# Second products with tokens stationary in the 768-token tiles, four low halves per tile on GpSimd, and the cubic term in another instruction form

## The chip, the core and the metric

The kernel runs on one core of one Trainium2 chip. The metric is device time in microseconds (us), from the start of the program to its end, as the median of several runs; the profile adds one execution seen instruction by instruction.

## The reference, cut to what matters

2,304 tokens of width 512 come out of a local and global attention (4 batches, 8 heads, 512 local and 32 global tokens each) and go through two feed-forward layers with 2,048 hidden units. The change touches the second layer.

```
x = moe(attention(...))                       # layer 1: h = relu(x @ w_in); x = (h*h) @ w_out
h = x @ w_in                                  # layer 2, (2304, 512) @ (512, 2048)
P = a[0] + a[1]*h + a[2]*h*h + a[3]*h*h*h
Q = 1.0 + |b[0]|*|h| + |b[1]|*h*h
out = (P / (Q + 1e-6)) @ w_out                # (2304, 2048) @ (2048, 512)
```

## The kernel before

Each float32 number that enters TensorE is split into a high half (rounded to the fp32r type) and a low half (the remainder), and each product is made of three matmuls: high by high, high by low, low by high.

Most of the tokens of both layers are worked in six tiles (SUMMED): three in layer 1 and three in layer 2, of 768, 768 and 640 tokens (numbers 3, 4 and 5 of the list). A tile's first product, x @ w_in, is a Strassen-like scheme: seven products M1 to M7 of half-size blocks (`product`, line 438), whose moving operands are seven sums of blocks of the tile, named A11, A12, S2, S1, S3, A22 and S4. `sides` makes those sums, their high halves (ScalarE, line 336) and their low halves (VectorE, line 339), a step at a time, for the next tile while the present one is worked. The last four low halves are those of S1, S3, A22 and S4. A tile has eight rounds (q, NPAIR of them; s counts them over all tiles), each for two chunks (f) of 128 hidden units. The program of a round is written out by hand in `step_a` to `step_d`: the products M1; M2 and M6; M5 and M7; M4 and M3. They go to two banks of PSUM, s0 and s1. After each of these four steps, `groups` puts in one part of the second product of an earlier round (six parts, one and a half rounds, late).

VectorE adds the parts of the seven products together (lines 627, 659 and 684: one operand in SBUF, one in PSUM, and the bank can be written again when they have read it), and it does most of the rational function of the round before (lines 547 to 572): `below`, `cube`, `above`, `error`, `ratio`, `refine`, and `glow`, which makes the low half of the result for the second product. These instructions read both inputs from SBUF. ScalarE does the squares, the logarithm and exponential for the division, the high halves and many copies out of PSUM. GpSimd in layer 2 does no arithmetic: it issues the fetches (`fetch`, line 416) of the weight blocks of the round after next, each of which waits until TensorE has read the block that it overwrites. The order on each engine is the order of the program.

The second product, g @ w_out (`blocks`, line 465), accumulates a whole tile over 16 chunks. In tiles 3 and 4, as in layer 1, the weight is the stationary operand and the tokens move: for each of four strips of 128 output columns, a matmul over 512 tokens and one over 256, in the banks tc0, tc1, pv0, pv1 (512) and s2, s3 (two pieces of 256 each); three matmuls to each piece, 24 to a chunk, in two parts. `leave` then copies eight pieces out of PSUM, on ScalarE for these tiles, and four DMAs write the tile to the output with columns and tokens transposed; the host puts it right. In the last tile (5) the tokens are the stationary operand, 128 at a time, and all 512 output columns of the weight move: five rows of 128 tokens, three matmuls of 512 columns each, in tc0, tc1, pv0, pv1 and s2; `depart` copies each row out and writes it.

Of the kernel before, what the change touches and what calls it, by code (L numbers as in the profile page):

```python
# [11 lines left out]
F32 = mybir.dt.float32  # L12
# [5 lines left out]
ALU = mybir.AluOpType  # L18
# [4 lines left out]
DM, DFF = 512, 2048  # L23
NTOK = B * (SL + SG)
# [13 lines left out]
KD, KF = DM // 128, DFF // 128  # L38
# [3 lines left out]
SUMMED = [(512, 256), (1024, 256), (1536, 320), (0, 384), (768, 384), (1536, 320)]  # L42
NPAIR = KF // 2
LAST = len(SUMMED) - 1
# [38 lines left out]

def body(ctx, tc, qT, kW, v, w1i, w1o, w2i, w2o, coef, out):
    nc = tc.nc
    cut = SUMMED[LAST][0]
    out_t = out[:cut * DM].rearrange("(p d c) -> p d c", p=128, d=KD)
    out_r = out[cut * DM:].rearrange("(n c) -> n c", c=DM)
    pe, act, dve, pool, sync = nc.tensor, nc.scalar, nc.vector, nc.gpsimd, nc.sync

    assert nc.sbuf_base <= BASE
# [4 lines left out]
    def at(name, off, *shape, dt=F32):  # L96

        assert off % 16 == 0 and off + int(np.prod(shape)) <= END * (2 if dt == I64 else 1)
        uses[name] = uses.get(name, 0) + 1
        return nc.alloc_sbuf_tensor_at(f"{name}_{uses[name]}", [128, *shape], dt, offset=BASE + 4 * off)[:]  # L100

    class Ring:
# [5 lines left out]
        def next(self):  # L108
            self.turn += 1
            return self.all[(self.turn - 1) % len(self.all)]  # L110
# [6 lines left out]
    x = at("x", 0, KD, NTOK)  # L117
# [19 lines left out]
    s_ps = [ps.tile([128, 512], F32, name=f"s{j}") for j in range(4)]  # L137
# [3 lines left out]
    acc_bank = tc_ps + pv_ps  # L141
# [148 lines left out]
    got = [[at("got", W0 + 8960 + 3584 * i + a, b - a, dt=F32R) for a, b in zip(CUTS, CUTS[1:])] for i in range(2)]  # L290
# [30 lines left out]
    def halves(t, part):  # L321
        p = pieces(t)
        n = len(p) // 2
        return p[n * part:n * part + n]

    def side(c, t, k):
        return sides_b[t][SLOTS[t][c]][k]

    def sides(t):

        c0, n = SUMMED[t]
        p11, p12, p21, p22 = (x[:, 2 * k:2 * k + 2, c0 + i * n:c0 + i * n + n] for i in range(2) for k in range(2))
        f = side("S2", t, 2)

        def high(c, src):
            act.activation(side(c, t, 0), src, AF.Copy)

        def low(c, src):
            dve.tensor_tensor(side(c, t, 1), src, side(c, t, 0).bitcast(F32), op=ALU.subtract)

        def sub(o, a, b, op=ALU.subtract):
            dve.tensor_tensor(o, a, b, op=op)

        high("A11", p11)
        yield
        low("A11", p11)
        yield
        sub(p11, p11, p21)
        high("A12", p12)
        yield  # L350
        low("A12", p12)
        yield
        sub(f, p22, p11)
        yield
        sub(p21, p21, p22, ALU.add)
        high("S2", f)
        yield
        sub(p12, p12, f)
        yield
        low("S2", f)  # L360
        yield
        high("S1", p21)
        high("S3", p11)
        low("S1", p21)
        yield
        high("A22", p22)
        low("S3", p11)
        yield
        high("S4", p12)
        low("A22", p22)  # L370
        yield
        low("S4", p12)
        yield

    def sides_now(t):

        c0, n = SUMMED[t]
        p11, p12, p21, p22 = (x[:, 2 * k:2 * k + 2, c0 + i * n:c0 + i * n + n] for i in range(2) for k in range(2))
        f = side("S2", t, 2) if t < 3 else at("sf", RAW + 7680, 2, n)
        src = {"A11": p11, "A12": p12, "S2": f, "S1": p21, "S3": p11, "A22": p22, "S4": p12}  # L380

        def high(c):
            act.activation(side(c, t, 0), src[c], AF.Copy)

        def low(c):
            dve.tensor_tensor(side(c, t, 1), src[c], side(c, t, 0).bitcast(F32), op=ALU.subtract)

        def sub(o, a, b, op=ALU.subtract):
            dve.tensor_tensor(o, a, b, op=op)

        def early():
            high("A11")
            yield
            low("A11")
            yield
            sub(p11, p11, p21)
            high("A12")
            yield
            low("A12")
            yield  # L400
            sub(f, p22, p11)
            yield
            sub(p21, p21, p22, ALU.add)
            yield
            sub(p12, p12, f)
            high("S2" if t < 3 else "S4")
            yield
            low("S2" if t < 3 else "S4")
            yield

        return early(), high, low
# [27 lines left out]
                          skip_group_check=True)  # L439

    def rows(t):
        return acc_bank + s_ps[2:4 if SUMMED[t][1] == 384 else 3]

    def part_of(t, part):
        return (range(3), range(3, len(rows(t))))[part]

    def blocks(q, f, part):

        t, u = divmod(q, NPAIR)
        j = u + NPAIR * f  # L450
        gh, gl = gq[q, f]
        w = w_out[j]
        assert have[1, j] == (q >= Q2)
        if t < LAST:
            pp = halves(t, part)
            ops = [(dst, w[:, a, 128 * d:128 * d + 128], b[:, o0:o1], first and i == 0, i == 2)
                   for d, o0, o1, dst, first in pp for i, (a, b) in enumerate(((0, gh), (1, gh), (0, gl)))]
        else:
            ops = [(rows(t)[k], b[:, 128 * k:128 * k + 128], w[:, a], i == 0, i == 2)
                   for k in part_of(t, part) for i, (a, b) in enumerate(((0, gh), (1, gh), (0, gl)))]  # L460
            if q == NQ - 1:
                order = ((0, 1, 3, 4, 6, 7, 2, 5, 8), (0, 1, 2, 3, 4, 6, 7, 5, 8))[f] if part == 0 else (0, 1, 3, 4, 2, 5)
                ops = [ops[i] for i in order]
        for dst, a, b, first, final in ops:
            pe.matmul(dst, a, b, start=first and j == 0, stop=j == KF - 1 and final, skip_group_check=True)  # L465
        if part == 1 and t == 2:
            freed.add(j)
        if j == KF - 1:
            (leave if t < LAST else depart)(t, part)
        for work in after.pop((q, f, part), ()):  # L470
            work()

    def leave(t, part):
        c0 = SUMMED[t][0]
        for k, (d, o0, o1, src, _) in enumerate(halves(t, part)):
            dst = x[:, d, c0 + o0:c0 + o1]
            if k % 2 == 0 and not (t in (3, 4) or t == 2 and part == 1):
                dve.tensor_copy(dst, src)
            else:
                act.activation(dst, src, AF.Copy)  # L480
            if t >= 3 and k % 2 == 1:
                sync.dma_start(out_t[:, d, c0:c0 + o1], x[:, d, c0:c0 + o1])

    def depart(t, part):
        c0, n = SUMMED[t]
        for k in part_of(t, part):
            rest = x[:, :, c0 + 512:c0 + 2 * n]
            o = x[:, k, c0:c0 + 512] if k < 4 else rest[:, 2 * (k - 4):2 * (k - 4) + 512 // (2 * n - 512)]
            i, r = rows(t)[k], out_r[128 * k:128 * k + 128]
            if k >= 4:  # L490
                i, r = (b.rearrange("p (a b) -> p a b", b=2 * n - 512) for b in (i, r))
            if t == len(SUMMED) - 1 and k % 2:
                dve.tensor_copy(o, i)
            else:
                act.activation(o, i, AF.Copy)
            (act if t == len(SUMMED) - 1 and k == len(rows(t)) - 1 else sync).dma_start(r, o)

    b2, b3 = 4 * Q2, 4 * NQ
    plan = {(Q2, 1): (), (Q2, 2): (b2 + 1,), (Q2, 3): (b2 + 2, b2 + 3),
# [7 lines left out]
    def group(i):  # L507
        i -= 6
        if i == 4 * Q2:
            return  # L510
        q, r = divmod(i - (i > 4 * Q2), 4)
        if 0 <= q < NQ:
            blocks(q, *divmod(r, 2))
# [19 lines left out]
    def ew(q, f):  # L533
        return [e[:, :2 * half(q)] for e in ea[f]] + [strip(q, 2 + f), strip(q, f)]
# [13 lines left out]

    def cube(q, f):
        a, b, t, h = ew(q, f)  # L550
        dve.tensor_tensor(t, t, h, op=ALU.mult)  # L551

    def above(q, f):
        a, b, t, h = ew(q, f)
# [28 lines left out]
    def step_a(s, tick):  # L583
# [16 lines left out]
        if two:  # L600
            linear(p, 0)
            cube(p, 0)
# [10 lines left out]
        if two:  # L613
            above(p, 0)
            below(p, 1)
            if not lagging(s):
                cube(p, 1)
            logexp(p, 0)
# [315 lines left out]
    with tc.manual_schedule():  # L934
# [12 lines left out]
        for a in range(2):  # L947
            h = m[64 * a:64 * a + 64]
# [6 lines left out]
        for b, r, c in ((0, 64, 0), (2, 0, 0), (3, 64, 128)):  # L955
            o = 32 * (b % 2)
# [504 lines left out]
        first, high, low = sides_now(0)  # L1461
# [48 lines left out]
        for q in range(1, Q2):  # L1510
            t, u = divmod(q, NPAIR)
            if q == NPAIR:
                spend(0.1)
            for k, step in enumerate((step_a, step_b, step_c, step_d)):
# [10 lines left out]
                if (u, k) == ((6, 0) if t < 2 else (5, 1)):  # L1525
                    if t:
                        clear(*((5, 6, 7) if t == 1 else (8, 9, 10, 1, 2, 3)))
                    early, high, low = sides_now(t + 1)
# [16 lines left out]
                if t == 0:  # L1545
# [4 lines left out]
                    while convs and (q, k) >= open_from[0] and owed > 0:  # L1550
                        c = next(convs[0], None)
# [96 lines left out]
```

## Time and profile before

| | |
|---|---|
| Median of 3 runs | 836.68 us (836.37 to 836.82) |
| The profiled execution | 836.86 us, of which the span shown is 835.1 us |
| TensorE (PE) busy | 827.8 us, 99% |
| VectorE (DVE) busy | 710.7 us, 85% |
| ScalarE (ACT) busy | 637.3 us, 76% |
| GpSimd (POOL) busy | 187.6 us, 22% |
| Granted clock of TensorE | 1.00 |

Busy time is what the profiler records for instructions; a matmul's recorded time overlaps with that of the next, so the pace of TensorE is read from starts, not from busy time. The profiled execution is 1.8 us longer than its span, and 0.18 us longer than the median.

### The profile page before, as it was taken

The page shows a single profiled execution, that of the slowest core. Times are in us where ns is not written, and L with a number is a line of the kernel's source. Part 1 is how long each engine was busy: PE and PEld are TensorE (multiplying, and loading weights), DVE is VectorE, ACT ScalarE, POOL GpSimd, SP SyncE. Part 2 cuts the span into 40 slices and gives each one's busy share as a digit, 9 for nine tenths or more (in the row PEclk, how much of TensorE's full clock was granted, in tenths as well). Part 3 has the DMA queues.
Part 4 walks back from the last instruction along what each step waited for, and adds up shares of the span by engine and source line. Part 5 has one row for each costly group of instructions (what it writes and reads, how often), then busy time and mean ns, then how long its engine had stood idle before and what let it go on. Part 6 is the DMA issues. An engine that isn't in the chain of part 4 may idle for free.

```text
span 835.1 us, 15580 instructions
## 1 busy us (share of the span) xinstructions
PE 827.8 (99%) x5671; PEld 742.0 (89%) x5671; DVE 710.7 (85%) x1424; ACT 637.3 (76%) x1244; POOL 187.6 (22%) x352
## 2 busy tenths in 40 slices
PE   9999999999999999999999999999999999999997
PEld 5888888888899998999999999999999999899995
DVE  5788889997787477687788699999999999989997
ACT  6899968875767576776777788878887878888775
POOL 4677766650000111111111121111111111111100
PEclk9999999999999999999999999999999999999999
DMA  9797579924598789899986474344364334365401
GB/s 349 277 331 259 215 271 413 398 103 151 208 328 297 267 261 402 291 325 374 371 262 191 143 243 127 114 114 129 107 189 121 120 114 122 120 214 150 144 11 64
DMA packets 50829, 181.38 MB, mean 217 GB/s; under 512 B 5696, under 2 KB 8512, under 8 KB 49856
## 3 DMA queue, kind: packets, MB, share of 16 engines
q1 hardware_dynamic: 31264, 100.94, 32.1%
q0 software_dynamic: 18960, 79.18, 30.7%
q8 instruction: 45, 0.74, 0.3%
q10 hardware_dynamic: 528, 0.26, 0.1%
q14 instruction: 32, 0.26, 0.1%
HBM read 139.73 MB, written 40.63 MB: 216 GB/s over the span
## 4 chain that ended last, share of the span: by engine, by line
PE 88%; DVE 9%; ACT 1%; DMA 1%; issue 0%; SPq 0%; ACTq 0%
PE s L438 32%; PE pv L465 13%; PE tc L465 13%; PE s L465 8%; PE s L239 5%; PE pv L848 3%; PE tc L249 3%; PE pv L249 3%; PE s L775 3%; PE tc L827 3%; PE pv L854 2%; DVE x L551 1%; DVE x L555 1%; DVE g L531 1%; DVE e L547 1%; PE s L899 1%
## 5 line engine op out<-in xcount | busy, mean ns | idle before, releaser
L438 PE MATMUL s<-sh,got 128*128 128x320 f32 (+2 forms) x1120 | 279.0, 315 | 0.6 <-DVE x L627 0.6
L438 PEld LDWEIGHTS s<-sh,got 128*128 128x128 f32 x1120 | 196.8, 189 | 4.7 <-DVE x L627 1.0
L416 POOL DMA_DIRECT2D got<-pr x120 | 64.9, 541 | 536.9 <-PE s L438 512.7
L438 PE MATMUL s<-sl,got 128*128 128x320 f32 (+2 forms) x560 | 176.0, 314 | 0.0
L465 PE MATMUL tc<-g,w 128*128 128x512 f32 (+1 forms) x480 | 127.2, 383 | 0.2 <-DVE g L531 0.2
L465 PE MATMUL pv<-g,w 128*128 128x512 f32 (+1 forms) x480 | 126.5, 382 | 0.0
L438 PEld LDWEIGHTS s<-sl,got 128*128 128x128 f32 x560 | 105.7, 189 | 2.3
L465 PEld LDWEIGHTS s<-g,w 128*128 128x128 f32 x576 | 93.6, 188 | 11.0
L465 PE MATMUL s<-g,w 128*128 128x256 f32 x576 | 98.7, 280 | 0.0
L465 PEld LDWEIGHTS tc<-g,w 128*128 128x128 f32 x480 | 83.1, 188 | 9.8 <-DVE g L531 1.4
L465 PEld LDWEIGHTS pv<-g,w 128*128 128x128 f32 x480 | 83.3, 188 | 8.4
L527 ACT ACTIVATE g<-x 128x512 fp32r<-128x512 f32 (+2 forms) x95 | 69.7, 734 | 15.1 <-DVE x L572 13.1
L531 DVE TENSOR_TENSOR g<-x,g 128x512 fp32r<-128x512 f32 (+2 forms) x95 | 77.6, 817 | 1.0 <-ACT g L527 0.9
L806 POOL TENSOR_SCALAR sm<-sm,rs 128x160 f32<-128x160 f32 x128 | 55.4, 459 | 30.2 <-DVE x L882 19.2
L792 ACT ACTIVATE sm<-sm,nm 128x160 f32<-128x160 f32 x128 | 55.6, 444 | 7.6 <-DVE nm L784 7.1
L547 DVE SCALAR_TENSOR_TENSOR e<-e,nf,e 128x768 f32<-128x768 f32 (+1 forms) x48 | 46.5, 968 | 10.5 <-ACT e L539 10.5
L652 ACT ACTIVATE u<-s 128x256 f32<-128x256 f32 (+2 forms) x48 | 21.0, 437 | 42.2 <-PE s L438 42.2
L784 DVE CUSTOM_DVE_ANT_0 sm<-s,mask 128x160 f32<-128x160 f32 x128 | 36.1, 321 | 15.4 <-PE s L775 12.1
L194 POOL TENSOR_TENSOR w<-cv,w 128x512 fp32r<-128x512 f32 x32 | 42.2, 1321 | 30.8 <-ACT w L188 24.7
L543 ACT ACTIVATE x<-x,nf 128x768 f32<-128x768 f32 (+1 forms) x48 | 47.1, 982 | 0.0
L678 ACT ACTIVATE x<-s 128x256 f32<-128x256 f32 (+2 forms) x48 | 21.0, 438 | 34.1 <-PE s L438 32.3
L555 DVE SCALAR_TENSOR_TENSOR x<-x,nf 128x768 f32<-128x768 f32 (+1 forms) x48 | 46.4, 966 | 0.4
(202 smaller groups left out, 1780.1 us busy)
## 6 DMA issues: line engine op xcount, KB each, us to landing
got<-pr POOLq DMA_DIRECT2D x80, 512.0 KB, 3.9
got<-pr POOLq DMA_DIRECT2D x40, 768.0 KB, 4.7
pr<-half SPq DMA_DIRECT2D x24, 512.0 KB, 5.6
v<-in_v_dram SPq DMA_DIRECT2D x7, 1408.0 KB, 8.4
k<-in_kW_dram SPq DMA_DIRECT2D x15, 592.0 KB, 6.2
r<-in_w1i_dram SPq DMA_DIRECT2D x16, 512.0 KB, 9.1
r<-in_w1o_dram SPq DMA_DIRECT2D x16, 512.0 KB, 11.1
pr<-tw SPq DMA_DIRECT2D x16, 512.0 KB, 3.6
```

Source lines behind the costliest of these rows:

```text
L194: pool.tensor_tensor(w[:, 1], f, w[:, 0].bitcast(F32), op=ALU.subtract)
L249: pe.matmul(acc_bank[d][:, :n], w[:, half, 128 * d:128 * d + 128], src[:, :n], start=start, stop=stop)
L416: pool.dma_start(got[q % 2][k], pairs[q >= Q2][q % NPAIR][:, o0:o1])
L438: pe.matmul(bank(q, i), a[:, k], b[:, k], start=first and k == 0 and j == 0, stop=k == 1 and j == 2, skip_group_check=True)
L465: pe.matmul(dst, a, b, start=first and j == 0, stop=j == KF - 1 and final, skip_group_check=True)
L527: act.activation(gpair(q, f)[0], strip(q, 2 + f), AF.Copy)
L531: eng.tensor_tensor(gl, strip(q, 2 + f), gh.bitcast(F32), op=ALU.subtract)
L543: act.activation(t, h, AF.Identity, scale=nf[:, 3:4], bias=nf[:, 2:3])
L547: dve.scalar_tensor_tensor(a, in0=a, scalar=nf[:, 5:6], in1=b, op0=ALU.mult, op1=ALU.add)
L555: dve.scalar_tensor_tensor(t, in0=t, scalar=nf[:, 1:2], in1=h, op0=ALU.add, op1=ALU.mult)
L792: act.activation(e, e, AF.Exp, scale=-1.0, bias=nm[:, k:k + 1], accum_out=tot[:, k:k + 1])
L806: pool.tensor_scalar(e, e, rs[:, k:k + 1], 1.0, op0=ALU.mult, op1=ALU.mult)
```

## The change

Three edits. In `blocks`, tiles 3 and 4 take the form of the last tile: 128 tokens are stationary and the 512 output columns move, in six rows with three matmuls of 512 columns each, three rows to a part; the banks are used in the order tc0, tc1, s2, pv0, pv1, s3 (for the 640-token tile tc0, tc1, s2, pv0, pv1). `depart` copies the rows out (on ScalarE for tiles 3 and 4) and writes them with one DMA each, untransposed. In `sides`, which serves tiles 4 and 5, the low halves of S1, S3, A22 and S4 are made by GpSimd, at the same places of the program. In `cube`, the tensor_tensor of two inputs becomes a scalar_tensor_tensor with a factor of 1.0.

```diff
-        def low(c, src):
-            dve.tensor_tensor(side(c, t, 1), src, side(c, t, 0).bitcast(F32), op=ALU.subtract)
+        def low(c, src, eng=dve):
+            eng.tensor_tensor(side(c, t, 1), src, side(c, t, 0).bitcast(F32), op=ALU.subtract)
...
-        low("S1", p21)
+        low("S1", p21, pool)
...
-        low("S3", p11)
+        low("S3", p11, pool)
...
-        low("A22", p22)
+        low("A22", p22, pool)
...
-        low("S4", p12)
+        low("S4", p12, pool)
...
     def rows(t):
-        return acc_bank + s_ps[2:4 if SUMMED[t][1] == 384 else 3]
+        return acc_bank[:2] + s_ps[2:3] + acc_bank[2:] + s_ps[3:4 if SUMMED[t][1] == 384 else 3]
...
-        if t < LAST:
+        if t < 3:
...
-            (leave if t < LAST else depart)(t, part)
+            (leave if t < 3 else depart)(t, part)
...
-            if k % 2 == 0 and not (t in (3, 4) or t == 2 and part == 1):
+            if k % 2 == 0 and not (t == 2 and part == 1):
...
-            if t >= 3 and k % 2 == 1:
-                sync.dma_start(out_t[:, d, c0:c0 + o1], x[:, d, c0:c0 + o1])
...
-            i, r = rows(t)[k], out_r[128 * k:128 * k + 128]
+            i, r = rows(t)[k], out_r[c0 + 128 * k:c0 + 128 * k + 128]
...
     def cube(q, f):
         a, b, t, h = ew(q, f)
-        dve.tensor_tensor(t, t, h, op=ALU.mult)
+        dve.scalar_tensor_tensor(t, in0=t, scalar=1.0, in1=h, op0=ALU.mult, op1=ALU.mult)
```

## Rows read from the trace of the kernel before

**Rows 1.** The page's first part: each engine's busy time, share, instructions.

```profile
PE 827.8 (99%) x5671; PEld 742.0 (89%) x5671; DVE 710.7 (85%) x1424; ACT 637.3 (76%) x1244; POOL 187.6 (22%) x352
```

**Rows 2.** Windows around the two tile changes: length, then busy time by engine.

```profile
564.00:600.00 36.00, 35.55 (x204) 32.92 (x203) 35.31 (x43) 30.06 (x41) 3.79 (x7) 1.00 0.39 117
690.00:730.00 40.00, 39.62 (x234) 36.24 (x233) 39.14 (x50) 33.95 (x48) 4.33 (x8) 1.00 0.40 122
```

**Rows 3.** Waits of TensorE's matmuls from 376 us on: total, times, longest.

```profile
PE s L438 <- DVE x L627: 0.6, 2, 0.4
```

**Rows 4.** Critical chain at the change from tile 3 to 4: start, length.

```profile
578.20 0.87 DVE sl L339
...
586.20 1.74 DVE sl L339 x2
...
590.66 0.47 DVE x L627
591.18 2.35 PE s L438 x12
```

**Rows 5.** Critical chain at the change from tile 4 to 5.

```profile
711.76 1.47 DVE sl L339 x2
...
722.15 0.88 DVE g L531
...
723.07 0.50 PE tc L465
```

**Rows 6.** Timeline of GpSimd late in the first layer's weight preparation.

```profile
177.46 1.30 POOL L194 TENSOR_TENSOR w<-cv,w 128x512 fp32r<-128x512 f32 x1 [2.32 <-ACT w L188]
...
182.90 3.00 POOL L194 TENSOR_TENSOR w<-cv,w 128x512 fp32r<-128x512 f32 x2 [2.32 <-ACT w L188]
```

**Rows 7.** Timeline of VectorE at the same time, and one earlier.

```profile
113.02 0.69 DVE L279 TENSOR_TENSOR gl<-b,gh 128x512 fp32r<-128x512 f32 x1 [2.58 <-ACT gh L275]
...
178.03 1.28 DVE L279 TENSOR_TENSOR gl<-b,gh 128x512 fp32r<-128x512 f32 x1
...
184.67 1.51 DVE L1189 TENSOR_TENSOR fw<-fw,fw 128x256 f32<-128x256 f32 x1
186.22 0.42 DVE L1190 TENSOR_TENSOR fw<-fw 128x256 f32<-128x256 f32 x1
```

**Rows 8.** Timeline of GpSimd in the attention, alone and beside VectorE's three-operand form.

```profile
57.53 1.58 POOL L806 TENSOR_SCALAR sm<-sm,rs 128x160 f32<-128x160 f32 x4 [1.11 <-DVE x L882]
...
105.45 2.37 POOL L806 TENSOR_SCALAR sm<-sm,rs 128x160 f32<-128x160 f32 x3
```

**Rows 9.** Timeline of VectorE at the second of those places.

```profile
105.84 1.40 DVE L172 SCALAR_TENSOR_TENSOR cv<-r,cv 128x512 int32<-128x512 int32 x2
```

**Rows 10.** Critical chain: one part of a second product in tile 3, weights stationary.

```profile
605.03 0.70 PE tc L465 x3
...
607.12 2.08 PE s L438 x12
```

**Rows 11.** Critical chain: one part of a second product in tile 5, tokens stationary.

```profile
763.49 1.39 PE tc L465 x6
764.88 0.68 PE pv L465 x3
```

**Rows 12.** Groups by line and form, from 520 us on: busy, mean ns.

```profile
L551 DVE TENSOR_TENSOR x<-x 128x768 f32<-128x768 f32 x26 | 24.7, 949 | 0.0
L564 DVE SCALAR_TENSOR_TENSOR e<-e,e 128x768 f32<-128x768 f32 x26 | 24.6, 948 | 0.0
L480 ACT ACTIVATE x<-s 128x256 f32<-128x256 f32 x8 | 3.1, 385 | 0.5 <-PE s L465 0.5
L480 ACT ACTIVATE x<-pv 128x512 f32<-128x512 f32 x4 | 2.4, 590 | 0.0
```

**Rows 13.** DMA issues of layer 2: KB each, median us to landing.

```profile
got<-pr POOLq DMA_DIRECT2D x41, 512.0 KB, 3.8
out_dram<-x SPq DMA_DIRECT2D x8, 384.0 KB, 3.2
```

More of the change, by code (lines that the diff above doesn't have):

```diff
@@ L85, in body @@
     nc = tc.nc
-    cut = SUMMED[LAST][0]
-    out_t = out[:cut * DM].rearrange("(p d c) -> p d c", p=128, d=KD)
-    out_r = out[cut * DM:].rearrange("(n c) -> n c", c=DM)
+    out_r = out.rearrange("(n c) -> n c", c=DM)
     pe, act, dve, pool, sync = nc.tensor, nc.scalar, nc.vector, nc.gpsimd, nc.sync
@@ L488, in depart @@
             o = x[:, k, c0:c0 + 512] if k < 4 else rest[:, 2 * (k - 4):2 * (k - 4) + 512 // (2 * n - 512)]
-            i, r = rows(t)[k], out_r[128 * k:128 * k + 128]
+            i, r = rows(t)[k], out_r[c0 + 128 * k:c0 + 128 * k + 128]
             if k >= 4:
                 i, r = (b.rearrange("p (a b) -> p a b", b=2 * n - 512) for b in (i, r))
-            if t == len(SUMMED) - 1 and k % 2:
+            if t == LAST and k % 2:
                 dve.tensor_copy(o, i)
@@ L495, in depart @@
                 act.activation(o, i, AF.Copy)
-            (act if t == len(SUMMED) - 1 and k == len(rows(t)) - 1 else sync).dma_start(r, o)
+            (act if t == LAST and k == len(rows(t)) - 1 else sync).dma_start(r, o)
     b2, b3 = 4 * Q2, 4 * NQ
@@ L1641 @@
     r = run_bass_kernel_spmd(nc, [arrays], core_ids=[0])
-    got, cut = np.asarray(r.results[0]["out_0_dram"]), SUMMED[LAST][0]
-    got = np.concatenate([got[:cut * DM].reshape(128, KD, cut).transpose(2, 1, 0).reshape(cut, DM),
-                          got[cut * DM:].reshape(NTOK - cut, DM)])
+    got = np.asarray(r.results[0]["out_0_dram"]).reshape(NTOK, DM)
     loc = got[:B * SL].reshape(B, SL // 256, 4, 64, DM)[:, :, [1, 0, 2, 3]].reshape(B, SL, DM)
```

## The prediction

> **What bounds the kernel now.** The page's first part comes first: TensorE is busy 99% of the span [rows 1], and VectorE, with 85%, is the next. A busy TensorE need not be at its peak, so the windows and the chain of waits come second. Around the two changes of tile in layer 2, and nowhere else in its middle, TensorE has idle time in the windows: 36.00 - 35.55 = 0.45 us and 40.00 - 39.62 = 0.38 us [rows 2]. VectorE is busy there 35.31 of 36 and 39.14 of 40 us. The waits say for what: most of it is L627, the VectorE addition that frees bank s1 for product M5 [rows 3]. The chain shows how that comes about: up to TensorE's product at 591.18 it runs through VectorE alone [rows 4]; at the second change TensorE's second product at 723.07 follows on VectorE's low half of g [rows 5]. In these two stretches VectorE has a little more work than time, because low halves of the next tile (line 339) fall on it; the last four of them, of which S1's at 578.20 and the two at 586.20 stand in [rows 4], are those that the change moves. So two things decide: the pace of TensorE's stream of matmuls, and how long VectorE is held in two stretches of some 25 us.
>
> **The second product.** Weights stationary, one part costs 607.12 - 605.03 = 2.09 us for 12 matmuls with 2,304 + 2,304 = 4,608 columns: six of 512, six of 256 [rows 10]. Tokens stationary, nine matmuls of 512 are again 4,608 columns, and tile 5 shows six in 1.39 and three in 0.68 us, 2.07 us together [rows 11]. By the six alone it would be 2.085. There are 2 tiles x 16 chunks x 2 parts = 64 parts: 64 x 0.02 = 1.3 us saved at most, 0.3 at least. I take 0.8, the middle, since the rows read at 0.01 us. Fewer loads of stationary data (18 for 24 in a chunk) save nothing more: the stream is already set by columns.
>
> **Leaving PSUM.** Eight copies on ScalarE (4 x 0.590 + 4 x 0.385 = 3.9 us a tile) become six (6 x 0.590 = 3.5) [rows 12]: 0.4 us less on an engine that TensorE does not wait for. The banks are needed again only after TensorE's next parts, so I cost it at nothing. If that cover were gone, the difference would be in favour of the change. On SP's queue six DMAs of 256 KB replace four of 384 KB that land in 3.2 us [rows 13]; nothing reads the output, and SP has nothing else queued behind them. Nothing.
>
> **The cubic term.** Two-input form 949 ns, three-operand form with a constant 948 ns, on the same 768 elements [rows 12]. 32 + 16 instructions by 1 ns: nothing.
>
> **The four low halves, first on VectorE.** It loses four instructions a tile. At the first change each takes 0.87 us of the chain, four 3.5 [rows 4]; at the second two take 1.47, so 0.73 each, four 2.9 [rows 5]. Were that all, TensorE's idle 0.45 + 0.38 = 0.83 us [rows 2] would go.
>
> **Then on GpSimd.** GpSimd's subtraction of 512 elements takes 1.30 us [rows 6]. The question is what VectorE can do meanwhile. The rows of layer 1's weight preparation show it. VectorE's two-input subtraction takes 0.69 us when GpSimd is idle; at 178.03, inside GpSimd's 177.46 to 178.76, it takes 1.28 and ends 0.55 us after GpSimd [rows 6, 7]. It stood still until GpSimd was nearly done. The case that matters more is a VectorE that never pauses: of the pair from 182.90 the second GpSimd subtraction ends at 185.90, and VectorE's 256-element subtraction of 184.67, which followed another at once, took 1.51 us where its sister at 186.22 took 0.42 [rows 6, 7]. GpSimd got in between two back-to-back instructions, and VectorE lost 1.51 - 0.42 = 1.09 us. The three-operand form is no shelter: beside two of them (1.40 us together) three GpSimd scalings took 2.37 us, where four take 1.58 alone [rows 8, 9]. They exclude each other too.
>
> The Trainium skill has this as a rule (SBUF — State Buffer, section Who interferes with whom): a VectorE instruction with two SBUF inputs and a GpSimd instruction that reads SBUF share a port under an exclusive lock, for the whole instruction, and issue order rather than the kind of operation decides who blocks. The traces above agree. By that rule the move makes VectorE later, not earlier; without it, the move gains.
>
> At both changes nearly all of VectorE's instructions read two SBUF inputs (lines 531 to 572); only the additions L627, L659 and L684, some 0.47 us each [rows 4], read one. So each moved low half holds VectorE for GpSimd's time. No row shows a GpSimd subtraction of 768 or 640. From 1.09 us for 512, by elements: 1.64 and 1.36 us. Upper bound by the full recorded 1.30: 1.95 and 1.63. Lower bound zero, if GpSimd always falls into gaps. I take 1.64 and 1.36, since VectorE's stream has hardly a gap. Net per low half: 1.64 - 0.87 = +0.77, four +3.1 us at the first change; 1.36 - 0.73 = +0.63, four +2.5 at the second. At each change I let one hold fall on an addition that reads PSUM and runs on beside it: -0.47 and, by elements (320 for 384), -0.40. That leaves +2.6 and +2.1 us.
>
> Does it reach TensorE? All four fall before the L627 at 590.66 on which M5 waits [rows 4]: on VectorE they stood between 578.20 and 586.20 + 1.74, so what they read is there by then. GpSimd's queue allows it, since behind these instructions are only fetches for the round after next, which land in 3.8 us [rows 13] and have a round to spare, which is four parts and three and a half steps of products, 4 x 2.09 + 3.5 x 2.08 = 15.6 us [rows 10]. VectorE has no slack between, so its delay comes out in full at L659, at the low half of g or at L627, whichever is latest. What is queued behind the moved instructions on GpSimd costs nothing; what waits behind a held VectorE is the whole rational function, and TensorE after it. After the change of tile VectorE recovers as before.
>
> **The sum.** Against the profiled execution: 836.86 + 2.6 + 2.1 - 0.8 = 840.8; it ran 0.18 above the median, so 840.6 us, +0.47%. The bounds: with full holds 4 x (1.95 - 0.87) + 4 x (1.63 - 0.73) = 7.9, less 0.3, gives 844.3; with two holds covered at each change and 1.3 saved, +2.1 + 1.7 - 1.3 = 2.5, 839.2. The likeliest case's own range is 839.2 to 844.3.
>
> **Rivals.** *GpSimd finds its gaps.* VectorE's relief of 3.5 and 2.9 us is real and the holds are covered, because a busy VectorE keeps GpSimd out and it works in pauses before and after the stretch. Then 0.83 us of idle time goes, and 0.8 of matmuls: 836.68 - 1.6 = 835.1; with 1.3 of matmuls 834.5. For it: S1's low half has from 578.20 to 591.18, 13 us, before TensorE needs it [rows 4], and beside the three-operand form it was GpSimd that waited longest [rows 8]. Against it: the 1.51 us [rows 7]. It decides if a hold costs VectorE less than 0.87 us at the first change and 0.73 at the second.
>
> *GpSimd gets in only at the additions from PSUM.* Each hold then overlaps 0.47 or 0.40 us of allowed work: (1.64 - 0.47 - 0.87) x 4 = 1.2 and (1.36 - 0.40 - 0.73) x 4 = 0.9; less 0.8, +1.3: 838.0.
>
> *The low halves come too late.* VectorE keeps GpSimd waiting so long that S4's low half is not there for the step of M4 and M3, which comes at 591.18 + 2.35 + 2.09 = 595.6 [rows 4, 10], 8 us after the last one's old place. TensorE then waits for GpSimd itself. If each change loses 3 to 4 us so, 836.68 + 7 - 0.8 = 842.9. Against it: GpSimd's four need 4 x 1.95 = 7.8 us in all, and they can begin before 578.20.
>
> **Chances.** Holds on VectorE (840.6) 0.55; additions only (838.0) 0.15; gaps (835.1) 0.24; too late (842.9) 0.06. About 0.2%, 1.7 us, is what a measurement of this kernel can tell from no change. The first and last are slower, the second mostly within (I give 0.04 of it to slower), and the third lies at the edge: 0.14 faster, 0.10 within. So faster 0.14, same 0.21, slower 0.65. The range must take in the gap case, which alone holds more than 2 in 10: 834.4, a little under that case's lower figure, up to the first's upper bound, 844.3.
>
> **What the profile after would show.** GpSimd has eight subtractions a little before and after 578 and 586 and the same at the second change, four each, of 1.6 us or longer. If I am right, VectorE instructions beside them (lines 551 to 572 and 531) show 1.5 us and more in place of 0.95, no matter which form, and TensorE's idle time around the two changes grows from 0.83 us to five or six. If VectorE's durations stay at 0.95 and GpSimd's grow, the gap case holds. A part of the second product should take 2.07 to 2.09 us, with no other wait at PSUM's banks. A wait of TensorE for GpSimd would show the fourth case. The prediction fails if a hold is shorter than the instruction it replaces, or if matmuls with stationary tokens run faster than tile 5 shows.

## The result, and the profile after

The changed kernel takes 842.25 us (median of 6 runs, 841.96 to 843.34) against 836.7 us: a ratio of 1.0068, 95% interval 1.0057 to 1.0079. It is slower by 5.6 us; 840.6 was forecast, with 839.2 to 844.3 as the range of that case. The profiled execution took 842.12 us, with a span of 840.3.

The page's first part, which answers to [rows 1]:

```profile
PE 828.6 (99%) x5479; PEld 733.1 (87%) x5479; DVE 715.0 (85%) x1416; ACT 637.4 (76%) x1240; POOL 205.5 (24%) x360
```

The windows around the two changes of tile, which answer to [rows 2] (length; busy time and instructions of PE, PEld, DVE, ACT and POOL; granted clock, DMA share, GB/s):

```profile
564.00:600.00 36.00, 33.20 (x164) 29.04 (x163) 35.23 (x36) 27.23 (x37) 12.95 (x10) 1.00 0.37 112
690.00:730.00 40.00, 37.75 (x189) 32.50 (x189) 39.09 (x43) 29.90 (x42) 12.96 (x12) 1.00 0.38 108
```

TensorE idles 36.00 - 33.20 = 2.80 and 40.00 - 37.75 = 2.25 us, 5.05 in all, where it was 0.83. VectorE is as busy as before but gets fewer instructions done: 36 in the first window for 43, 43 in the second for 50. Of the seven fewer in each, four are the moved ones; the rest did not fit. GpSimd is busy 12.95 us for 3.79, and 12.96 for 4.33.

The waits of TensorE's matmuls from 376 us on (total, times, longest), which answer to [rows 3]; lines 527, 603 and 623 are 531, 607 and 627 of before:

```profile
PE tc L463 <- DVE g L527: 2.4, 3, 1.4
PE s L436 <- DVE x L623: 1.7, 2, 0.9
PE s L436 <- ACT u L603: 0.9, 2, 0.5
```

Two of the three releasers are VectorE's. The third, a copy of ScalarE out of bank s0, is VectorE at one remove: among ScalarE's own waits from 480 us on its copy of the high half of g waits for VectorE's `refine` 18.8 us in all (longest 3.6) where it had waited 13.1 (longest 1.9), and the copies are queued behind it. One more wait, 0.2 us for ScalarE, is in the last tile and was there before. None is for GpSimd, for a fetch or for a bank of the second product.

Now the first change of tile itself. The timeline of GpSimd (start, length; L337 is the moved subtraction, L414 the fetch):

```profile
576.11 3.73 POOL L337 TENSOR_TENSOR sl<-x,sh 128x768 fp32r<-128x768 f32 x1 [9.55 <-ACT sh L334]
579.78 0.59 POOL L414 DMA_DIRECT2D got<-pr  x1
580.39 1.96 POOL L337 TENSOR_TENSOR sl<-x,sh 128x768 fp32r<-128x768 f32 x1
582.30 1.11 POOL L414 DMA_DIRECT2D got<-pr  x2
583.43 1.86 POOL L337 TENSOR_TENSOR sl<-x,sh 128x768 fp32r<-128x768 f32 x1
588.73 2.21 POOL L337 TENSOR_TENSOR sl<-x,sh 128x768 fp32r<-128x768 f32 x1 [3.44 <-ACT sh L334]
```

And that of VectorE:

```profile
575.37 1.01 DVE L564 SCALAR_TENSOR_TENSOR x<-x,nf,e 128x768 f32<-128x768 f32 x1
...
577.17 0.95 DVE L568 SCALAR_TENSOR_TENSOR x<-e,x 128x768 f32<-128x768 f32 x1
578.04 0.55 DVE L655 TENSOR_TENSOR x<-u,s 128x384 f32<-128x384 f32 x1
578.50 2.15 DVE L564 SCALAR_TENSOR_TENSOR x<-x,nf,e 128x768 f32<-128x768 f32 x1
580.58 2.59 DVE L527 TENSOR_TENSOR g<-x,g 128x768 fp32r<-128x768 f32 x1
583.09 3.03 DVE L568 SCALAR_TENSOR_TENSOR x<-e,x 128x768 f32<-128x768 f32 x1
586.04 0.54 DVE L680 TENSOR_TENSOR x<-u,s 128x384 f32<-128x384 f32 x1
...
587.43 0.95 DVE L527 TENSOR_TENSOR g<-x,g 128x768 fp32r<-128x768 f32 x1
...
589.28 2.47 DVE L551 SCALAR_TENSOR_TENSOR x<-x,nf 128x768 f32<-128x768 f32 x1
...
593.94 1.01 DVE L551 SCALAR_TENSOR_TENSOR x<-x,nf 128x768 f32<-128x768 f32 x1
```

Each GpSimd subtraction has one VectorE instruction beside it that takes 2 to 3 us in place of 0.95 or 1.01, the length of the same instruction without GpSimd beside it (575.37, 577.17, 587.43, 593.94), and that ends 0.8 us after GpSimd does: 580.65 after 579.84, 583.17 after 582.35, 586.12 after 585.29, 591.75 after 590.94. They are of both forms. What such an instruction loses by standing still is called its hold here. What they lost: 1.14, 1.64, 2.08 and 1.46, together 6.32 us; the four low halves that VectorE no longer makes saved 4 x 0.87 = 3.48 [rows 4]. Net +2.84. At the second change the four are these:

```profile
707.62 1.86 DVE L564 SCALAR_TENSOR_TENSOR x<-x,nf,e 128x768 f32<-128x768 f32 x1
709.41 2.32 DVE L527 TENSOR_TENSOR g<-x,g 128x768 fp32r<-128x768 f32 x1
711.65 2.75 DVE L568 SCALAR_TENSOR_TENSOR x<-e,x 128x768 f32<-128x768 f32 x1
...
717.57 2.19 DVE L551 SCALAR_TENSOR_TENSOR x<-x,nf 128x768 f32<-128x768 f32 x1
```

Beside the third of them is the shortest of GpSimd's subtractions there:

```profile
711.99 1.58 POOL L337 TENSOR_TENSOR sl<-x,sh 128x640 fp32r<-128x640 f32 x1
```

Lost 0.85 + 1.37 + 1.80 + 1.18 = 5.20, saved 4 x 0.73 = 2.92 [rows 5], net +2.28. The two together are 5.1 us, and the span grew by 840.3 - 835.1 = 5.2.

The second product's pace, from the chain of waits while tile 4's first product runs in the changed kernel (start, length), answers to [rows 10]; the last two lines are the products M1 that open two rounds:

```profile
605.85 2.10 PE s L436 x12
607.96 1.39 PE tc L463 x6
609.35 0.69 PE s L463 x3
610.04 2.10 PE s L436 x12
...
618.41 1.06 PE s L436 x6
...
634.12 1.06 PE s L436 x6
```

And the two M1 that open the same rounds in the kernel before:

```profile
615.47 1.04 PE s L438 x6
...
631.12 1.04 PE s L438 x6
```

One part is 610.04 - 607.96 = 2.08 us, where it was 2.09; but the step of 12 product matmuls beside it is 2.10 or 2.11, where it was 2.08. Part and step together take 4.19 in place of 4.17 us, and a whole round, from one M1 to the next, 15.71 in place of 15.65. What I had booked as a saving is not there.

### The profile page after: what moved, and what is told of

The parts are those of the page before. It is cut to its first block, busy times and chain, and to the rows that moved or that the text cites. A ratio compares the mean times of both kernels' runs of the same rounds, so it can differ in the third digit from the quotient of the medians.

```text
span 840.3 us, 15208 instructions
## 1 busy us (share of the span) xinstructions
PE 828.6 (99%) x5479; PEld 733.1 (87%) x5479; DVE 715.0 (85%) x1416; ACT 637.4 (76%) x1240; POOL 205.5 (24%) x360
## 4 chain that ended last, share of the span: by engine, by line
PE 88%; DVE 9%; ACT 1%; DMA 1%; issue 0%; SPq 0%; ACTq 0%
PE s L436 31%; PE pv L463 13%; PE tc L463 13%; PE s L463 8%; PE s L237 5%; PE pv L844 3%; PE s L771 3%; PE pv L247 3%; PE tc L247 3%; PE tc L823 2%; PE pv L850 2%; DVE x L551 1%; DVE g L527 1%; DVE x L547 1%; DVE x L564 1%; DVE x L568 1%
## 5 line engine op out<-in xcount | busy, mean ns | idle before, releaser
L414 POOL DMA_DIRECT2D got<-pr x120 | 65.0, 542 | 498.5 <-PE s L436 418.1
L523 ACT ACTIVATE g<-x 128x512 fp32r<-128x512 f32 (+2 forms) x95 | 69.8, 734 | 20.8 <-DVE x L568 18.8
L463 PE MATMUL tc<-w,g 128*128 128x512 f32 x288 | 75.8, 395 | 2.6 <-DVE g L527 2.4
L463 PE MATMUL pv<-w,g 128*128 128x512 f32 x288 | 74.3, 393 | 0.0
L463 PE MATMUL tc<-g,w 128*128 128x512 f32 (+1 forms) x288 | 72.1, 376 | 0.0
L463 PE MATMUL pv<-g,w 128*128 128x512 f32 (+1 forms) x288 | 71.7, 375 | 0.0
L463 PE MATMUL s<-w,g 128*128 128x512 f32 x240 | 68.4, 392 | 0.0
L463 PEld LDWEIGHTS tc<-w,g 128*128 128x128 f32 x288 | 52.5, 188 | 13.2 <-DVE g L527 4.0
L463 PEld LDWEIGHTS pv<-w,g 128*128 128x128 f32 x288 | 53.1, 188 | 8.7
L463 PEld LDWEIGHTS tc<-g,w 128*128 128x128 f32 x288 | 49.8, 189 | 6.2 <-DVE g L527 0.6
L463 PEld LDWEIGHTS pv<-g,w 128*128 128x128 f32 x288 | 50.0, 189 | 5.6
L463 PEld LDWEIGHTS s<-w,g 128*128 128x128 f32 x240 | 45.1, 188 | 10.2
```

Source lines behind the costliest of these rows:

```text
L414: pool.dma_start(got[q % 2][k], pairs[q >= Q2][q % NPAIR][:, o0:o1])
L523: act.activation(gpair(q, f)[0], strip(q, 2 + f), AF.Copy)
```

## The experiments

Ten kernels ran, each compared with runs of the kernel before on the same chip (its median lay between 836.66 and 836.97 us; differences between two of the ten that ran on different chips carry these 0.3 us). The theory on record: GpSimd's reads hold VectorE, and this costs more than the work taken off VectorE. Its rivals: that other edits carry part of the loss, that what matters is where GpSimd's work stands in its queue, or that any use of SBUF by GpSimd does it.

### The parts of the change alone

The low halves back on VectorE, all else as changed:

```diff
-        low("S1", p21, pool)
+        low("S1", p21)
```

and the same for S3, A22 and S4.

> The changed kernel with the four low halves back on VectorE; the new form of the second product and of the cubic term stay. Theory (GpSimd's reads hold VectorE, and nothing else of the change costs): the 5 us go, 836.6 to 837.3 us; a part of the second product and its neighbours cost what they cost before, so the 0.8 us that I had booked as saved do not show. Rival (the tokens-stationary form, through its loads or its banks, is part of the loss): above 839.

Measured: 837.23 us, ratio 1.0005 (0.9996 to 1.0013). TensorE's idle time is back at 0.37 and 0.40 us:

```profile
564.00:600.00 36.00, 35.63 (x177) 31.69 (x176) 35.26 (x44) 29.67 (x41) 3.78 (x7) 1.00 0.42 117
690.00:730.00 40.00, 39.60 (x204) 34.85 (x204) 39.09 (x50) 33.35 (x47) 3.91 (x8) 1.00 0.43 124
```

So the new second product, the new way out of PSUM and the three-operand form are together worth nothing that can be measured; if anything 0.6 us the wrong way. The forecast saving of 0.8 us, a ratio of 0.9990, lies outside the interval. The other way round, the kernel before with the four low halves on GpSimd and nothing else:

```diff
-        def low(c, src):
-            dve.tensor_tensor(side(c, t, 1), src, side(c, t, 0).bitcast(F32), op=ALU.subtract)
+        def low(c, src, eng=dve):
+            eng.tensor_tensor(side(c, t, 1), src, side(c, t, 0).bitcast(F32), op=ALU.subtract)
...
-        low("S1", p21)
+        low("S1", p21, pool)
```

> The kernel before with one edit, the four low halves on GpSimd; second product and cubic term as before. Theory: the whole loss, 841.5 to 842.5 us, with VectorE instructions of 2 to 3 us at both changes of tile. Rival (the loss needs the other edits too, for instance the three-operand cubic term or the late second product): 836 to 839.

Measured: 841.8 us, ratio 1.0061 (1.0049 to 1.0074), and the held instructions at the first change take 2.15, 2.59, 3.02 and 2.47 us. The whole loss is in this edit, within the noise. The cubic term in its old form, the rest as changed:

```diff
-        dve.scalar_tensor_tensor(t, in0=t, scalar=1.0, in1=h, op0=ALU.mult, op1=ALU.mult)
+        dve.tensor_tensor(t, t, h, op=ALU.mult)
```

> The changed kernel with the cubic term as the two-operand instruction again. Theory (two SBUF inputs are two SBUF inputs): 842.0 to 842.5 us, no difference. Rival (VectorE's three-operand form keeps GpSimd out, the two-operand form lets it in, so that holds come earlier or are longer): 843 or more.

Measured: 842.14 us, ratio 1.0063 (1.0049 to 1.0077), and the held instructions take 2.15, 2.59, 3.03 and 2.47 us, to the digit what they take in the changed kernel. The form is worth nothing here. In neither of the two kernels is it a cubic term that is held.

### Is it GpSimd's reading?

GpSimd copies the block where it subtracted: one input read, not two. The low half is then the block itself and not the remainder.

```diff
-            eng.tensor_tensor(side(c, t, 1), src, side(c, t, 0).bitcast(F32), op=ALU.subtract)
+            if eng is pool:
+                pool.tensor_copy(side(c, t, 1), src)
+            else:
+                eng.tensor_tensor(side(c, t, 1), src, side(c, t, 0).bitcast(F32), op=ALU.subtract)
```

> The changed kernel, but GpSimd copies the block into the low half instead of subtracting: one input read in place of two, so the low half is not the remainder. Theory (VectorE loses the time in which GpSimd reads): GpSimd about 1.0 us an instruction, holds of about 0.8 us against 0.87 saved, 836.5 to 837.5 us. Rival (the loss is GpSimd's place in the order, its fetches or its semaphores, whatever it does): 840 or more.

Measured: 836.02 us, ratio 0.9992 (0.9983 to 1.0001), a little under what was expected. In the timelines of GpSimd and of VectorE a copy takes 0.84 us, and the VectorE instruction beside it 1.65 in place of 0.95:

```profile
572.96 0.84 POOL L338 CAST sl<-x 128x768 fp32r<-128x768 f32 x1
```

```profile
572.98 1.65 DVE L550 SCALAR_TENSOR_TENSOR x<-x 128x768 f32<-128x768 f32 x1
```

A hold of 0.70 us against 0.87 saved: the hold is shorter than the instruction it replaces. Against 837.23 us, all four on VectorE, the move now gains 1.2 us; from the kernel before it can't be told. A copy need not wait for the high half, so S1's and S3's run 7 us earlier than the subtractions and S4's 5, and this run alone does not separate shorter reading from the earlier place. The last two copies, with the addition and the instruction beside them, are these:

```profile
582.62 1.60 POOL L338 CAST sl<-x 128x768 fp32r<-128x768 f32 x2
```

```profile
582.60 0.55 DVE L683 TENSOR_TENSOR x<-u,s 128x384 f32<-128x384 f32 x1
583.28 1.76 DVE L546 SCALAR_TENSOR_TENSOR e<-e,nf,e 128x768 f32<-128x768 f32 x1
```

The addition L683, one input in SBUF and one in PSUM, keeps its length beside a reading GpSimd; L546, with two inputs in SBUF, is held. Then GpSimd writes and reads nothing; the low halves are zeros, and their products are left out:

```diff
-            eng.tensor_tensor(side(c, t, 1), src, side(c, t, 0).bitcast(F32), op=ALU.subtract)
+            if eng is pool:
+                pool.memset(side(c, t, 1).bitcast(F32), 0.0)
+            else:
+                eng.tensor_tensor(side(c, t, 1), src, side(c, t, 0).bitcast(F32), op=ALU.subtract)
```

> The changed kernel, but GpSimd only writes zeros into the four low halves: it reads nothing, and the low halves are left out of the products. Theory (what holds VectorE is GpSimd's reading): VectorE's instructions beside the fills keep 0.95 to 1.01 us, TensorE's idle time at the changes of tile goes, 835.5 to 836.5 us. Rival (any GpSimd access to SBUF holds VectorE): VectorE instructions beside a fill are longer by the fill's time, though the total can still be near 836.

Measured: 835.6 us, ratio 0.9982 (0.9973 to 0.9991). The timelines show two fills of 0.72 us each and the same L546 in the midst of them, at its usual length:

```profile
582.52 1.44 POOL L338 MEMSET sl<- 128x768 f32 x2
```

```profile
582.81 1.02 DVE L546 SCALAR_TENSOR_TENSOR e<-e,nf,e 128x768 f32<-128x768 f32 x1 [0.64 <-ACT e L538]
583.75 0.95 DVE L530 TENSOR_TENSOR g<-x,g 128x768 fp32r<-128x768 f32 x1
```

The rival that any access holds VectorE is out: the fills stand where the copies stood (582.52 and 582.62), and reading holds VectorE, writing does not. The Trainium skill says the same (SBUF — State Buffer, section Who interferes with whom): a VectorE instruction with two SBUF inputs contends with a GpSimd instruction that reads SBUF, not with one that only writes it. This run also gives the worth of taking the four low halves off VectorE at no cost: 837.23 - 835.6 = 1.6 us, or 1.9 with each taken against the kernel before on its own chip.

### Does the loss add up by instruction?

S1 and S3 alone on GpSimd, and then A22 and S4 alone (each the changed kernel with `pool` left out of the other two calls).

> The changed kernel with only S1 and S3 on GpSimd; A22 and S4 are back on VectorE. Theory (the loss is the sum of holds less the work taken off VectorE, instruction by instruction): from the rows of the changed kernel 1.14 + 1.64 - 1.74 = 1.0 us at the first change and 0.85 + 1.37 - 1.47 = 0.75 at the second, about 1.8 us above the kernel with all four on VectorE, 838.5 to 839.3. Rival (VectorE absorbs two holds in its pauses, only four are too much): 837.2 or less.

Measured: 838.68 us, ratio 1.0022 (1.0013 to 1.0032), 1.45 above the kernel with all four on VectorE. VectorE's holds are those of the changed kernel, 2.15 and 2.59 us:

```profile
578.92 2.15 DVE L564 SCALAR_TENSOR_TENSOR x<-x,nf,e 128x768 f32<-128x768 f32 x1
580.99 2.59 DVE L527 TENSOR_TENSOR g<-x,g 128x768 fp32r<-128x768 f32 x1
583.50 0.94 DVE L568 SCALAR_TENSOR_TENSOR x<-e,x 128x768 f32<-128x768 f32 x1
```

> The changed kernel with only A22 and S4 on GpSimd; S1 and S3 are back on VectorE. Theory: 2.08 + 1.46 - 1.74 = 1.8 us and 1.80 + 1.18 - 1.47 = 1.5 us, about 3.3 above the kernel with all four on VectorE, 840 to 840.8; if the long hold of A22 (2.08) came from the two fetches issued just before it, which here are not together, it falls to 1.6 and the time to 839.5. Rival (holds late in the change of tile are covered): 838 or less.

Measured: 839.26 us, ratio 1.0029 (1.0018 to 1.0040), 2.03 above. A22's and S4's holds are now as long as S1's and S3's were, beginning behind the addition L680: A22's falls from 2.08 to 1.14 us, S4's rises from 1.46 to 1.65:

```profile
584.10 2.15 DVE L543 SCALAR_TENSOR_TENSOR e<-e,nf,e 128x768 f32<-128x768 f32 x1
586.18 2.60 DVE L527 TENSOR_TENSOR g<-x,g 128x768 fp32r<-128x768 f32 x1
```

The 840 to 840.8 that the expectation gave first took the holds from the changed kernel, and A22's did not stay; 839.5, for a shorter hold, was near. Two and two cost 1.45 + 2.03 = 3.5 us, all four 842.25 - 837.23 = 5.0. So two holds are not absorbed, against both rivals; but the four cost more than the two pairs added. The difference is in A22's hold, 0.94 us longer at each change when S1 and S3 run before it, less 0.2 of S4's. Without S1 and S3 its subtraction got in beside the addition L680; behind them it is on record from 583.43, after two fetches, beside an L568. The fetches themselves held nothing where it can be seen: the L568 of 583.50 above began while two fetches were being issued (the row for them in that run begins at 582.71 and lasts 1.11 us) and took 0.94 us.

### Can the idle time be had back without GpSimd?

The low half of S2 a round earlier, in the kernel before:

```diff
-            if phase == "a" and s > Q2 + 1:
-                pull(pending[0], 1 if u > 1 and s > Q2 + 3 else 2)
+            if phase == "a" and s > Q2 + 1 and u != NPAIR - 1:
+                pull(pending[0], 1 if u > 1 and s > Q2 + 3 and u != NPAIR - 2 else 2)
```

> The kernel before, with one edit: the low half of S2 (VectorE, as all of them) is made one round earlier, so that the last round before a change of tile has one low half less; nothing else moves. Theory (the idle time of TensorE at the changes is VectorE's surplus of work there, some 0.6 us each): 0.87 and 0.73 us less work there, idle time gone, 835.6 to 836.2 us. Rival (the round before has no pause for it either, or what TensorE waits for is something else): 836.6 or more.

Measured: 836.69 us, ratio 0.9998 (0.9989 to 1.0007). The rival was right. The wait of 0.6 us for L627 is gone, but TensorE now waits 0.3 us for another addition, L659: the round (M1 to M1 in TensorE's timeline) in which S2's low half now stands takes 16.29 us for 15.65. And all five spread out:

```diff
-            if phase == "a" and s > Q2 + 1:
-                pull(pending[0], 1 if u > 1 and s > Q2 + 3 else 2)
-            elif u == NPAIR - 1 and phase in "bc":
+            if phase == "a" and s > Q2 + 1 and u != NPAIR - 1:
+                pull(pending[0], 1 if u != 1 and s > Q2 + 3 and u != NPAIR - 2 else 2)
+            elif u == NPAIR - 1 and phase in "cd" or u == 0 and phase == "b":
```

> The kernel before, all low halves on VectorE, but spread further over the change of tile: S2 a round early, S1 after the third step in place of the second, S3 after the fourth, A22 after the next first, S4 after the next second. Three low halves in place of five then stand before the L627 on which TensorE waits. Theory (the idle time at the changes is VectorE's surplus there, and its place in the order decides): idle time 0.83 us goes to 0.2 or less, 835.5 to 836.3 us, at the edge of what can be told from the kernel before. Rival (VectorE's surplus only comes out at a later addition): 836.6 to 837.

Measured: 837.85 us, ratio 1.0014 (1.0005 to 1.0023): slower, if by little, and above what either side expected. The wait for L627 is gone, and in its place TensorE waits as long in all for another of VectorE's additions, L659:

```profile
PE s L438 <- DVE x L659: 0.6, 2, 0.3
```

The same spread in the kernel with tokens stationary, which has the other two edits of the change:

> The same spread, in the kernel with tokens stationary in the second product and the three-operand cubic term, all low halves on VectorE. Theory (these two edits are worth nothing either way): as the spread kernel within 0.6 us. Rival (tokens stationary is a little slower, as the 0.5 us of the first experiment hints): 0.4 to 0.8 us above the spread kernel.

Measured: 837.89 us, ratio 1.0012 (1.0003 to 1.0021), the same as the spread kernel; the half microsecond of the first experiment does not come back. My theory of the place in the order failed in both: moving a low half moves the wait to another addition and another round. By the lengths of the rounds the waits at the two changes cost 1.8 us before, 1.6 with S2's low half early and 2.5 with all five spread, there in four rounds in place of two. That is 0.7 of the 1.1 us by which the spread kernel is slower; the rest is open. No kernel that makes all of its low halves as the remainder beat the one before.

## Why the prediction was right

**What bounds the kernel.** Right. TensorE's idle time grew in the two stretches named, by 5.05 - 0.83 = 4.2 us, and nowhere else between 100 and 820 us; the span grew by 5.2. The rest stands in the lengths of the rounds. In TensorE's timeline of the changed kernel M1 starts at 567.53, 584.94 and 602.54 around the first change, rounds of 17.41 and 17.60 us where 15.71 is the length without a wait, and at 696.78, 713.51 and 730.39 around the second, 16.73 and 16.88 for 15.71 and 14.40 (the lengths without a wait are those of the kernel with fills). That is 7.1 us of waiting. The kernel before has 16.38 for 15.65 and 15.59 for 14.51, 1.8 us: 5.3 less. Idle time understates a wait: 0.45 us of it at 591.18 in the kernel before made its round 0.73 longer. With the 0.5 us of the second product below this is a little more than the span grew; tile 3's M1 at 489 us came 0.35 us earlier in the changed kernel's execution.

**The second product.** A term with the wrong sign: -0.8 forecast, +0.6 measured with the other two edits (837.23 against 836.66, an interval that takes in zero but not the saving). The step that failed is "tokens stationary, nine matmuls ... 2.07 us together": the part was 0.01 us shorter, but the product step between two parts became 0.02 to 0.03 longer, which I had not looked for. Rounds of 15.71 for 15.65 us, less what two shorter ones give back after the last change (14.40 for 14.51), make about +0.5 us over tiles 3 and 4, an estimate that fits the 0.6. Why the neighbours slow down was not tried. A price read in tile 5 held for the part and not for its neighbours.

**Leaving PSUM, the cubic term.** Nothing forecast for either; with the second product they came out as nothing within 0.1%, and the cubic term alone as nothing (842.14 against 842.25).

**The holds.** The mechanism as forecast: VectorE instructions of both forms stood still while GpSimd read, and the lot came out at TensorE. +4.7 us forecast for both changes, 842.25 - 837.23 = 5.0 measured; by rows 2.84 for 2.6 and 2.28 for 2.1. So of the 1.65 us between 840.6 and 842.25 some 1.4 belong to the second product and 0.3 to the holds. The range put on record, 834.4 to 844.3, took in the gains too; it is the rows, and not the number in its range, that bear the mechanism out. GpSimd's lengths, 1.86 and 1.58 us where nothing kept it back, lie under the upper bounds of 1.95 and 1.63. The loss in a back-to-back stream was taken as 1.64 from 512 elements, and one of the first change's four is 1.64, which is luck: the four run from 1.14 to 2.08, and it is their mean, 1.58 for the 1.52 forecast, that came out near. That one hold would fall beside an addition from PSUM is what S1's did at L655 (1.14). Two things in it were not as I had them. GpSimd did not get in at the next boundary: S1's subtraction began at 576.11 and lasted 3.73 us, 1.87 more than A22's, until the addition at 578.04 let it in. And A22's hold was 2.08, and 1.80 at the second change, over the upper bounds of 1.95 and 1.63: a hold can outlast GpSimd's recorded time.

**The rivals.** Gaps: refuted by the 2 and 3 us instructions. Its price was low too: with the waits gone the kernel with fills gains 1.6 to 1.9 us, where the idle time of 0.83 had been taken. Additions only: half true of S1, and of A22 when it was moved without S1 and S3, but the next subtraction each time held a whole instruction. Too late: no wait of TensorE for GpSimd, although S1 was kept waiting 1.9 us.

**Where TensorE waits.** L627 and the low half of g, as forecast; the 0.9 us for ScalarE's copy was not, and is the same delay come by way of ScalarE's queue. L659 released no matmul that counted.

## What to carry to other kernels

Before work is moved from VectorE to an idle GpSimd, look in the trace for a place where both ran at once, and price the move by what VectorE lost there, not by GpSimd's busy share: here a GpSimd subtraction of 768 elements cost VectorE 1.1 to 2.1 us to save it 0.87. The same move with an instruction that only writes cost VectorE nothing, and a copy, with one input read, held it 0.70 us. And where an engine has hardly a pause over several rounds, look at the rounds before and after: in the two changes of order tried here the wait moved and did not go.

## What the runs showed that was not expected

GpSimd can be kept out for several instructions: S1's subtraction waited while VectorE ran 576.30 to 578.04 without a pause, and got in beside an addition that reads PSUM; but the one that follows (580.39) got in between two instructions that read SBUF. The Trainium skill (SBUF — State Buffer, section Who interferes with whom) says that issue order decides who blocks. These rows show that a GpSimd already on record as started is not always the next to get in. What decides was not tried.

An instruction of VectorE that is on record as started before GpSimd's can be the one that stands still: L568 at 583.09 did so for GpSimd's subtraction on record from 583.43, and ended 0.83 us after it. Where two fetches stood without a subtraction behind them, the same L568 took 0.94 us. Whether GpSimd's claim is made earlier than its record begins is left open.
